# One unbroken TensorE visit per chunk for the recurrent part of a gated linear attention and gated MLP kernel

## Chip, cores and metric

One core of a Trainium2 chip. The metric is the device time of one launch in microseconds; the time shown for a kernel is the median of its runs.

## What is computed

Gated linear attention over 4 batches, 8 heads, 768 steps and head size 48, then a gated MLP with a convolution of three taps along the sequence ("MoE" in the code):

```
state = f[:, :, t, :, None] * state + einsum('bhd,bhe->bhde', k[:, :, t], v[:, :, t])   # f = sigmoid(f_logit)
y[:, :, t] = einsum('bhd,bhde->bhe', q[:, :, t], state)
...
h = maximum(x @ w_in, 0)                # x: y with the heads side by side, 384 wide; h: 1024 wide
conv_out = sum over k of conv_w[k] * hp[:, k:k+S, :]
out = (h * sigmoid(conv_out)) @ w_out
```

## The kernel before

The sequence is cut into 24 chunks of 128 steps, six to a batch. Chunk n goes through these steps; P is 128, NP the 4 pairs of heads, D the head size.

- `load_f`, `gate`, `load_kq`, `load_v` (lines 155 to 188): loads on SP's queue, and the logarithm of the gates on ScalarE (for later chunks three at a time, with a low part from GpSimd, line 175).
- `stage_a` (190): a matmul with a triangle sums the log gates (`pl`, 195), ScalarE takes both exponentials (199, 200), VectorE scales the keys (212), GpSimd the queries (213).
- `decay_out`, `decay_in` (216, 221): from chunk 5 on the last row of decays goes to DRAM and back, transposed, into `ft_all`.
- `stage_b` (229): four transposes each of keys and queries on TensorE (`ptk`, `ptq`, 235) and their copies out of PSUM into `kT` and `qT` (237): ScalarE, but for the keys of chunks 12 to 23 VectorE.
- `scores` (247): 8 matmuls of keys against queries, contraction 48, into `pa` (253); VectorE's masked copy into `am` (255).
- `state` (257): the rank update, 8 matmuls of keys against values into `pk` (266); VectorE adds the old state and multiplies with the decay (276, 277), which gives the state for chunk n+1. A batch's last chunk has none.
- `values` (279): the state part, 4 matmuls of state against queries (288; not at a batch's first chunk but the very first), and the score part, 8 matmuls of values against `am` (291), both summed in `py`. ScalarE and VectorE split the result in a high and a low part (299, 300) for the MLP.

Each matmul of plain fp32 is two instructions in the trace, so that a scores block is 16, a rank update 16, a state part 8, a score part 16, the transposes 4 and 4 (one instruction each).

The MLP works on half batches (three chunks). `mm1` (310): for each of 8 blocks of 128 hidden units a sum of 9 matmuls of 384 columns into `ph` (328), ScalarE's eviction (331), the convolution and the gate on both engines (333 to 343). `mm2` (345): for each 128 rows the high and low part of the gate's product (358, 359), a sum of 24 matmuls into `po` (365), eviction (368) and store (369). `ph` and `po` share two PSUM buffers; `pl`, `ptk`, `ptq` and `pk` share three; `pa` and `py` have one each.

The order of the work: every step is entered with a key by `plan` (383), mostly the chunk's number plus an offset of CFG, and is traced in the order of keys. The builder then goes through the traced program with its own model of times and gives each engine, whenever that is free, the instruction traced earliest among those whose inputs and buffers are ready in the model. The order on each engine is fixed by that when the kernel is built. A step that becomes ready can so come between two instructions of a step with a later key. On the chip each engine takes its instructions in this order and waits for semaphores.

The change touches `stage_b`, `scores`, `state`, `values` and the keys of lines 400 to 403. Before, these are:

```python
        plan(n - CFG["b"], lambda n=n: decay_out(n))          # b = 0.8
        plan(n - CFG["b"] + 0.4, lambda n=n: decay_in(n))
        plan(n, lambda n=n: scores(n))
        plan(n + CFG["s"], lambda n=n: state(n))              # s = 0.2
        plan(n + CFG["v"], lambda n=n: values(n))             # v = 0.5
```

The keys of `mm1` and `mm2` (lines 413 to 418) put the MLP of a half batch one to three half batches behind its attention; after the last chunk some MLP work remains alone.

Of the kernel before, what the change touches and what calls it, by code (L numbers as in the profile page):

```python
# [1 line left out]

# [7 lines left out]
F32 = mybir.dt.float32  # L10
# [7 lines left out]
P = 128  # L18
# [1 line left out]
F64_HI = float(np.uint32((1151 << 20) - 1).view(np.float32))  # L20

F_MIN = 2.0 ** -64
CFG = dict(groups=[3, 3, 3, 3, 3, 3, 3, 3], sg=3, f1=2.6, g1=2.6, gv=2, gl=5.2, g=3.9, l=3.2, a=1.8, b=0.8, s=0.2, v=0.5, wil=(-2.3, -1.1), wis=(-0.7, 0.9), cw=1.3, wol=(1.3, 1.0), wos=2.1, wo=0.35, m1=0.5, m1s=0.9, m2=1.5, m2s=1.2, ek=(12, 24), ec='d', er='p', tp=0, tf=2, nw=2, gd=0, q0=2, lf=3, kpool=2, eg='d', eq='p', es='d', em='d', ew='p', xb=3, nf=6, fe='a', kb=4, qb=3, vb=4, lv=2.2, cb=1, sb=3, fi=1)

@with_exitstack
def gla_moe_kernel(ctx, tc, q_in, k_in, v_in, f_in, w_in, conv_w, w_out, out):


    nc = tc.nc
    B, S, H, D = v_in.shape  # L30
    DM, DFF = w_in.shape
    q, k, v, f_logit = [t.rearrange("b s h d -> b h s d")[:, :, :, :D] for t in (q_in, k_in, v_in, f_in)]
    NC = S // P
    NP = H // 2
# [3 lines left out]
    CPH = NC // 2  # L38
    groups = CFG["groups"]
    GC = max(groups)  # L40
# [3 lines left out]
    HP = 64  # L44
# [7 lines left out]
    wk = fast.enter_context(tc.tile_pool(name="wk", bufs=2))  # L52
# [15 lines left out]
    mask = mask1.rearrange("p (j n t) -> p j n t", j=1, n=1).broadcast_to([P, 2, NP, P])  # L68

    def zeroed(shape, n, name, eng):  # L70
        ts = [wk.tile(shape, F32, name=f"{name}{i}", bufs=1) for i in range(n)]
        for t in ts:
            eng.memset(t, 0.0)
        return ts

    kp_b = [wk.tile([P, H, HP], F32, name=f"kp{i}", bufs=1) for i in range(CFG["kb"])]
    qp_b = [wk.tile([P, H, HP], F32, name=f"qp{i}", bufs=1) for i in range(CFG["qb"])]
    a_b = zeroed([P, 2, NP, P], 2, "am", nc.vector)
    s_b = zeroed([P, NP, HP + D], 2, "st", nc.vector)
# [6 lines left out]
    wo = const.tile([P, NF, 2, DM], F32R, name="wo")  # L86
    cw = const.tile([P, 3, NF], F32, name="cw")
# [30 lines left out]
    def raw_out(f):  # L118
        i = f // 4
        if ("o", i) not in raws:  # L120
            raws["o", i] = (wk.tile([P, 4, 2 * DM], I32, tag="g32", name=f"wos{i}") if i == 0 else
                            wk.tile([P, 4, 2 * DM], I32, tag="xT", name=f"wos{i}", bufs=CFG["xb"]))
        return raws["o", i][:, f % 4]
# [26 lines left out]

    last_exp = [None]
    group_of = [g for g, m in enumerate(groups) for _ in range(m)]
    ghl, gates, fbs, qkv, mid, tts, fts, ft_row = {}, {}, {}, {}, {}, {}, {}, {}

    def load_f(n):
        b, c = steps[n]
# [5 lines left out]
    def gate(g, i, m):  # L162

        if g >= CFG["lf"] and i == 0:
            ghl[g] = [wk.tile([P, GC, DM], F32R, tag=f"cg{x}", name=f"cg{x}{g}", bufs=CFG["cb"]) for x in "hl"]
        cs = slice(i * DM, (i + m) * DM)
# [49 lines left out]
    def decay_out(n):  # L216
        if n in fts:
            ft_row[n] = dr.tile([1, DM], F32, tag="ft", name=f"ft{n}", bufs=2)
            nc.sync.dma_start(ft_row[n], fts.pop(n)[P - 1:P].rearrange("o h d -> o (h d)"))

    def decay_in(n):

        if n in ft_row:
            b, c = steps[n]
            src = ft_row.pop(n).rearrange("o (p j d) -> j d (o p)", j=2, d=D)
            for j in range(2):
                nc.sync.dma_start(ft_all[HP * j:HP * j + D, b, c, :], src[j])

    def stage_b(n):
        qp, kp = mid.pop(n)  # L230
        tt = []
        for nm, src in (("k", kp), ("q", qp)):
            pt = ps.tile([P, NP, P], F32, tag="s", name=f"pt{nm}{n}", bufs=3)
            for p in range(NP):
                nc.tensor.transpose(pt[:, p, :], src[:, 2 * p:2 * p + 2, :].rearrange("p h d -> p (h d)"), ident)  # L235
            st = wk.tile([P, NP, P], F32, tag=f"{nm}T", name=f"{nm}T{n}")
            (nc.vector.tensor_copy if nm == "k" and CFG["ek"][0] <= n < CFG["ek"][1] else nc.scalar.copy)(st, pt)  # L237
            tt.append(st)
        tts[n] = (kp, tt[0], tt[1])

# [3 lines left out]
        nc.tensor.matmul(pw, zr[:, :P], zr, start=True, stop=True)  # L244
    xts = {}

    def scores(n):
        kp, kT, qT = tts[n]
        pa = ps.tile([P, 2, NP, P], F32, tag="A", name=f"pa{n}")
        for p in range(NP):  # L250
            for j in range(2):
                r = slice(HP * j, HP * j + D)
                nc.tensor.matmul(pa[:, j, p, :], kT[r, p, :], qT[r, p, :], start=True, stop=True)  # L253
        am = a_b[n % 2]
        nc.vector.copy_predicated(am, mask, pa)  # L255

    def state(n):
        b, c = steps[n]
        if c == NC - 1:
            return  # L260
        kp, kT, qT = tts[n]
        vt = qkv[n]
        pk = ps.tile([P, NP, D], F32, tag="s", name=f"pk{n}", bufs=3)
        for p in range(NP):
            for j in range(2):
                nc.tensor.matmul(pk[HP * j:HP * j + D, p, :], kp[:, 2 * p + j, :D], vt[:, 2 * p + j, :],  # L266
                                 start=True, stop=True)
        for j in range(2):
            r = slice(HP * j, HP * j + D)
            ft = ft_all[r, b, c, :].rearrange("p (n o) -> p n o", o=1).broadcast_to([D, NP, D])  # L270
            new = s_b[(n + 1) % 2][r, :, HP * j:HP * j + D]
            if c == 0:
                nc.vector.tensor_tensor(new, pk[r], ft, ALU.mult)
            else:
                tmp = wk.tile([P, NP, D], F32, tag="stmp", name=f"stmp{n}_{j}", bufs=1)
                nc.vector.tensor_tensor(tmp[r], pk[r], s_b[n % 2][r, :, HP * j:HP * j + D], ALU.add)
                (nc.vector if CFG["es"] == "d" else nc.gpsimd).tensor_tensor(new, tmp[r], ft, ALU.mult)

    def values(n):
        b, c = steps[n]  # L280
        kp, kT, qT = tts.pop(n)
        vt = qkv.pop(n)
        am = a_b[n % 2]
        py = ps.tile([P, NP, P], F32, tag="Y", name=f"py{n}")
        inter = c > 0 or n == 0
        if inter:
            for p in range(NP):
                nc.tensor.matmul(py[:HP + D, p, :], s_b[n % 2][:, p, :], qT[:, p, :], start=(p == 0), stop=False)  # L288
        for p in range(NP):
            for j in range(2):  # L290
                nc.tensor.matmul(py[HP * j:HP * j + D, p, :], vt[:, 2 * p + j, :], am[:, j, p, :],  # L291
                                 start=not inter and p == 0, stop=(p == NP - 1))
        hf = c // CPH
        if c % CPH == 0:
            xts[b, hf] = wk.tile([P, NP, 2, HS], F32R, tag="xT", name=f"xT{b}_{hf}", bufs=CFG["xb"])
        xT = xts[b, hf]
        ts = slice((c % CPH) * P, (c % CPH + 1) * P)
        for r in [slice(0, HP + D)] if c > 0 or n == 0 else [slice(0, D), slice(HP, HP + D)]:
            nc.scalar.copy(xT[r, :, 0, ts], py[r])  # L299
            nc.vector.tensor_tensor(xT[r, :, 1, ts], py[r], xT[r, :, 0, ts].bitcast(F32), ALU.subtract)  # L300
        if c % CPH == CPH - 1:
            for t in range(KT):
                for j in range(2):
                    s0, d0 = HP * j + GAP * t, HP * j + D
                    nc.sync.dma_start(xT[d0:d0 + GAP, t, :, :].bitcast(F32), xT[s0:s0 + GAP, KT, :, :].bitcast(F32))
# [77 lines left out]
    def plan(key, w):  # L383
        items.append((key, len(items), w))
# [10 lines left out]
    for n in range(N):  # L395
        plan(n - CFG["l"], lambda n=n: load_kq(n))
        plan(n - CFG["lv"], lambda n=n: load_v(n))
        plan(n - CFG["a"], lambda n=n: stage_a(n))
        plan(n - CFG["b"], lambda n=n: stage_b(n))
        plan(n - CFG["b"], lambda n=n: decay_out(n))  # L400
        plan(n - CFG["b"] + 0.4, lambda n=n: decay_in(n))
        plan(n, lambda n=n: scores(n))
        plan(n + CFG["s"], lambda n=n: state(n))
        plan(n + CFG["v"], lambda n=n: values(n))
    for i in range(DFF // WC):
        for kt in range(KT):
# [27 lines left out]
    with tc.If(n_ok < P * n_ft):  # L434
        with ExitStack() as slow:
            wk = slow.enter_context(tc.tile_pool(name="swk", bufs=2))
# [11 lines left out]
            st = wk.tile([P, DG, D], F32, name="sst", bufs=1)  # L448
            nc.gpsimd.memset(st, 0.0)
            for t0 in range(0, S, TB):  # L450
# [7 lines left out]
                fb, qb, kb = grouped(f_logit, "f"), grouped(q, "q"), grouped(k, "k")  # L458
                vb = wk.tile([P, TB, D], F32, tag="sv", name=f"sv{t0}")
# [22 lines left out]
                for t in range(0, TB, 8):  # L482
                    py = ps.tile([B * H, 8, D], F32, tag="sy", name=f"spy{t0}_{t}", bufs=2)
# [14 lines left out]
            for u in range(2 * B):  # L498
                b, hf = u // 2, u % 2
# [59 lines left out]
```

## Time and profile before

| what | us |
|---|---|
| median of 3 runs (lowest, highest) | 383.01 (381.41, 386.15) |
| the profiled execution, its own time | 384.77 |
| its span, first to last instruction | 383.1 |
| TensorE busy | 351.2 (92%) |
| TensorE loading weights | 313.2 (82%) |
| VectorE busy | 294.4 (77%) |
| ScalarE busy | 239.9 (63%) |
| GpSimd busy | 60.1 (16%) |

The profile is of one execution, and its rows below are from that. Busy matmul time is modelled from starts and sizes: a matmul that waits inside the array counts as busy. The time that a block costs is therefore read as the distance from its start to the start of the next block. PE is TensorE, PEld its weight loads, DVE VectorE, ACT ScalarE, POOL GpSimd, SP the engine that issues the transfers.

### The profile page before, as it was taken

The numbers are of one execution on the slowest core, as the hardware profiler recorded it, in microseconds if no ns is written. First come the engines' busy times: TensorE is split into PE (matmuls) and PEld (weight loads), VectorE is DVE, ScalarE is ACT, GpSimd is POOL, SyncE is SP. The second block draws the span as 40 slices with busy tenths as digits, with TensorE's granted clock in tenths as the row PEclk, the third lists the DMA queues.
The fourth block names the chain that finished last, engine by engine and source line by source line (L and its number), as shares of the span: only waits on it lengthen the run. The fifth ranks groups of instructions, "written<-read, shape, count | busy, mean of one in ns | idle before, by whom it ended". The sixth has DMA issues, their size and how long they took to land.

```text
span 383.1 us, 7239 instructions
## 1 busy us (share of the span) xinstructions
PE 351.2 (92%) x2735; PEld 313.2 (82%) x2735; DVE 294.4 (77%) x467; ACT 239.9 (63%) x426; POOL 60.1 (16%) x72
## 2 busy tenths in 40 slices
PE   5578799868989699999999999999999999999993
PEld 1557578746978599989989999999989899999993
DVE  3999999988989968667688896669869776575620
ACT  3687669993997376645875665547545555566530
POOL 1111134311103701104011121204101100000000
PEclk9989999996999989999999999999999999999998
DMA  7999253324334330132313332232201000201011
GB/s 224 347 366 362 83 164 105 89 59 104 105 76 108 75 114 21 50 90 87 113 56 99 75 81 83 69 87 74 66 22 34 21 2 21 54 21 43 21 44 49
DMA packets 28854, 36.04 MB, mean 94 GB/s; under 512 B 10847, under 2 KB 20106, under 8 KB 28810
## 3 DMA queue, kind: packets, MB, share of 16 engines
q1 hardware_dynamic: 28810, 35.49, 31.0%
q8 instruction: 24, 0.39, 0.4%
q14 instruction: 20, 0.16, 0.2%
HBM read 28.37 MB, written 4.75 MB: 86 GB/s over the span
## 4 chain that ended last, share of the span: by engine, by line
PE 60%; DVE 13%; ACT 9%; issue 5%; DMA 5%; POOL 3%; SPq 2%; ACTq 0%; POOLq 0%; DVEq 0%
PE po L365 23%; PE ph L328 21%; PE pa L253 4%; PE py L291 4%; DMA fb<-in_f_logit_dram 4%; PE py L288 3%; POOL cgl L175 3%; PE ptk L235 2%; PE ptq L235 1%; PE pl L195 1%; ACT fb L169 1%; DVE g L340 1%; PE pk L266 1%; ACT g L342 1%; DVE am L255 1%
## 5 line engine op out<-in xcount | busy, mean ns | idle before, releaser
L328 PE MATMUL ph<-xT,wi 128*128 128x384 f32 x576 | 116.4, 349 | 4.8 <-ACT hb L331 2.7
L328 PEld LDWEIGHTS ph<-xT,wi 128*128 128x128 f32 x576 | 100.0, 189 | 10.4 <-issue 3.9
L365 PE MATMUL po<-wo,gh 128*128 128x384 f32 x384 | 101.3, 345 | 0.0
L365 PEld LDWEIGHTS po<-wo,gh 128*128 128x128 f32 x384 | 69.9, 191 | 1.2 <-issue 0.7
L365 PE MATMUL po<-wo,gl 128*128 128x384 f32 x192 | 65.8, 343 | 1.3 <-DVE gl L359 1.3
L339 DVE SCALAR_TENSOR_TENSOR g<-hb,cw,g 128x384 f32<-128x384 f32 (+1 forms) x64 | 41.0, 640 | 15.5 <-ACT g L333 15.1
L359 DVE TENSOR_TENSOR gl<-g,gh 128x1024 fp32r<-128x1024 f32 (+4 forms) x34 | 31.4, 934 | 27.1 <-ACT gh L358 27.0
L331 ACT ACTIVATE hb<-ph 128x384 f32<-128x384 f32 x64 | 31.3, 489 | 31.3 <-PE ph L328 31.2
L213 POOL TENSOR_TENSOR qp<-qp,fd 128x384 f32<-128x384 f32 x22 | 31.5, 1430 | 99.4 <-ACT fd L200 95.0
L340 DVE SCALAR_TENSOR_TENSOR g<-hb,cw,g 128x384 f32<-128x384 f32 (+1 forms) x64 | 44.2, 690 | 1.9
L343 DVE SCALAR_TENSOR_TENSOR g<-g,hb 128x768 f32<-128x768 f32 (+1 forms) x32 | 31.4, 981 | 14.6 <-ACT g L342 14.3
L342 ACT ACTIVATE g<-g 128x768 f32<-128x768 f32 (+1 forms) x32 | 27.1, 848 | 24.3 <-DVE g L340 24.3
L358 ACT CAST gh<-g 128x1024 fp32r<-128x1024 f32 (+4 forms) x34 | 26.5, 800 | 23.7 <-PE po L365 20.6
L333 ACT ACTIVATE g<-hb,cw 128x384 f32<-128x384 f32 (+1 forms) x64 | 39.6, 618 | 2.0
L365 PEld LDWEIGHTS po<-wo,gl 128*128 128x128 f32 x192 | 36.6, 191 | 1.7 <-DVE gl L359 1.5
L253 PE MATMUL pa<-qT,kT 48*128 48x128 f32 x384 | 32.8, 298 | 1.2 <-ACT qT L237 1.1
L253 PEld LDWEIGHTS pa<-qT,kT 48*128 48x128 f32 x384 | 26.1, 195 | 9.5 <-issue 5.5
L255 DVE COPY_PREDICATED am<-mask,pa 128x1024 f32<-128x1024 uint8 x24 | 31.4, 1309 | 1.2 <-PE pa L253 1.1
L291 PE MATMUL py<-am,v 128*48 128x128 f32 x384 | 27.4, 284 | 1.1 <-DVE am L255 0.9
L288 PE MATMUL py<-qT,st 128*112 128x128 f32 x168 | 24.1, 283 | 2.6 <-DVE xT L300 1.6
L291 PEld LDWEIGHTS py<-am,v 128*48 128x48 f32 x384 | 20.6, 126 | 6.1 <-DVE am L255 2.0
L299 ACT CAST xT<-py 112x512 fp32r<-112x512 f32 (+1 forms) x27 | 15.8, 585 | 15.0 <-PE py L291 11.6
(92 smaller groups left out, 428.5 us busy)
## 6 DMA issues: line engine op xcount, KB each, us to landing
kp<-in_k_dram SPq DMA_DIRECT2D x24, 256.0 KB
qp<-in_q_dram SPq DMA_DIRECT2D x24, 256.0 KB
fb<-in_f_logit_dram SPq DMA_DIRECT2D x24, 192.0 KB
v<-in_v_dram SPq DMA_DIRECT2D x24, 192.0 KB
out_dram<-ob SPq DMA_DIRECT2D x24, 192.0 KB
wis<-in_moe_w_in_dram SPq DMA_DIRECT2D x6, 512.0 KB
wos<-in_moe_w_out_dram SPq DMA_DIRECT2D x8, 384.0 KB
xT<-xT SPq DMA_DIRECT2D x48, 48.0 KB
```

Of the source, the lines that this page charges most:

```text
L213: (nc.vector if CFG["eq"] == "d" or n < CFG["q0"] else nc.gpsimd).tensor_tensor(qp[:, :, :D], qp[:, :, :D], fd, ALU.mult)
L253: nc.tensor.matmul(pa[:, j, p, :], kT[r, p, :], qT[r, p, :], start=True, stop=True)
L255: nc.vector.copy_predicated(am, mask, pa)
L288: nc.tensor.matmul(py[:HP + D, p, :], s_b[n % 2][:, p, :], qT[:, p, :], start=(p == 0), stop=False)
L291: nc.tensor.matmul(py[HP * j:HP * j + D, p, :], vt[:, 2 * p + j, :], am[:, j, p, :], start=not inter and p == 0, stop=(p == NP - 1))
L328: nc.tensor.matmul(ph, wi[:, t, wl, f * P:(f + 1) * P], xts[b, hf][:, t, xl, :], start=(i == 0), stop=(i == 3 * KT - 1))
L333: nc.scalar.activation(cv, hb[:, 1:n + 1], AF.Copy, scale=cw[:, 1, f:f + 1])
L339: nc.vector.scalar_tensor_tensor(cv, hb[:, 2:n + 2], cw[:, 2, f:f + 1], cv, ALU.mult, ALU.add)
L340: nc.vector.scalar_tensor_tensor(cv, hb[:, 0:n], cw[:, 0, f:f + 1], cv, ALU.mult, ALU.add)
L343: nc.vector.scalar_tensor_tensor(cv, cv, 1.0, h_b[:, fp:fp + 2, 1:n + 1], ALU.add, ALU.mult)
L359: nc.vector.tensor_tensor(lo, g[:, f:f + k], hi.bitcast(F32), ALU.subtract)
L365: nc.tensor.matmul(po, g[:, f, :], wo[:, f, wl, :], start=(i == 0), stop=(i == 3 * NF - 1))
```

## The change

A visit of chunk n is made of the state part and score part of chunk n, the rank update of chunk n+1 and the scores of chunk n+1, in this order. From chunk 8 on (`ng`) the matmuls of each part are traced with a priority 4000 places ahead (`hp`). The first matmul of a visit gets a dependence on all copies into `kT` and `qT` of chunks n and n+1 and on the masked copy of chunk n; the first matmul of the rank update and of the scores gets an order edge, without a wait, behind the last matmul of the part before. `scores` and `state` of chunk n+1 get keys just behind `values` of chunk n. `decay_out` goes from 0.8 to 1.2 chunks ahead, `decay_in` from 0.4 to 0.7, for all chunks. The number of buffers of `kT` and `qT` becomes a setting (`tb`), at 2 as before.

```diff
-CFG = dict(groups=...
+CFG = dict(ng=8, hp=4000, tb=2, groups=...
...
-            st = wk.tile([P, NP, P], F32, tag=f"{nm}T", name=f"{nm}T{n}")
-            (nc.vector.tensor_copy if ... else nc.scalar.copy)(st, pt)
+            st = wk.tile([P, NP, P], F32, tag=f"{nm}T", name=f"{nm}T{n}", bufs=CFG["tb"])
+            i = (nc.vector.tensor_copy if ... else nc.scalar.copy)(st, pt)
+            ready.setdefault(n, []).append(i.ins)
...
+    NOSYNC = mybir.DependencyInfo(mybir.DependencyClass.NoSync, mybir.DependencyReason.DATA)
+    DATA = mybir.DependencyInfo(mybir.DependencyClass.Sync, mybir.DependencyReason.DATA)
+    last_pe = [None]
+
+    @contextmanager
+    def visit(n, part):
+        if n < CFG["ng"]:
+            yield
+            return
+        traced = nc.cur_bb.bb.instructions
+        start = len(traced)
+        with tc.high_priority(offset=CFG["hp"]):
+            yield
+        mine = traced[start:]
+        if part == 0:
+            for i in ready[n] + ready.get(n + 1, []):
+                tc.add_manual_dep(mine[0], i.name, DATA, reason="visit")
+        else:
+            tc.add_manual_dep(mine[0], last_pe[0].name, NOSYNC, reason="visit")
+        last_pe[0] = mine[-1]
...
     def scores(n):
-        for p in range(NP):
+        with visit(n - 1, 2):
+            for p in range(NP):
...
-        nc.vector.copy_predicated(am, mask, pa)
+        ready.setdefault(n, []).append(nc.vector.copy_predicated(am, mask, pa).ins)
...
     def state(n):
-        for p in range(NP):
+        with visit(n - 1, 1):
+            for p in range(NP):
...
     def values(n):
-        if inter:
+        with visit(n, 0):
+            if inter:
...
-        plan(n - CFG["b"], lambda n=n: decay_out(n))
-        plan(n - CFG["b"] + 0.4, lambda n=n: decay_in(n))
-        plan(n, lambda n=n: scores(n))
-        plan(n + CFG["s"], lambda n=n: state(n))
+        plan(n - 1.2, lambda n=n: decay_out(n))
+        plan(n - 0.7, lambda n=n: decay_in(n))
+        plan(n - 1 + CFG["v"] + 0.02 if n > CFG["ng"] else n, lambda n=n: scores(n))
+        plan(n - 1 + CFG["v"] + 0.01 if n > CFG["ng"] else n + CFG["s"], lambda n=n: state(n))
```

## Rows read from the trace of the kernel before

**Rows 1.** Two stretches: window, length, busy us of each engine, clock, DMA share, GB/s.
```profile
core 0: us, PE busy (x) PEld busy (x) DVE busy (x) ACT busy (x) POOL busy (x), PEclk, DMA share, GB/s
104.00:138.00 34.00, 29.34 (x232) 25.56 (x231) 31.76 (x48) 24.05 (x40) 11.05 (x8) 0.95 0.38 104
138.00:328.00 190.00, 189.81 (x1499) 174.66 (x1498) 145.39 (x207) 114.05 (x190) 27.31 (x34) 1.00 0.22 60
```

**Rows 2.** Waits of TensorE, 104 to 138 us: total us, times, longest us.
```profile
PE ptq L235 <- POOL qp L213: 1.7, 1, 1.7
PE po L365 <- DVE gl L359: 1.3, 1, 1.3
```

**Rows 3.** Waits of TensorE, 138 to 330 us, all of them.
```profile
PE ph L328 <- ACT ob L368: 0.2, 1, 0.2
```

**Rows 4.** Timeline of TensorE: start us, us, engine, line, what, count; whole blocks.
```profile
290.51 1.16 PE L253 MATMUL pa<-qT,kT 48*128 48x128 f32 x16
291.61 0.56 PE L266 MATMUL pk<-v,kp 128*48 128x48 f32 x16
292.10 0.66 PE L235 MATMUL ptk<-ident,kp 128*128 128x128 f32 x4
292.60 0.60 PE L235 MATMUL ptq<-ident,qp 128*128 128x128 f32 x4
```

**Rows 5.** Timeline of TensorE, a score part, then scores in two pieces.
```profile
245.63 1.08 PE L291 MATMUL py<-am,v 128*48 128x128 f32 x16
246.65 1.85 PE L328 MATMUL ph<-xT,wi 128*128 128x384 f32 x9
248.42 0.49 PE L253 MATMUL pa<-qT,kT 48*128 48x128 f32 x4
248.84 1.85 PE L328 MATMUL ph<-xT,wi 128*128 128x384 f32 x9
250.63 0.94 PE L253 MATMUL pa<-qT,kT 48*128 48x128 f32 x12
251.50 0.56 PE L266 MATMUL pk<-v,kp 128*48 128x48 f32 x16
```

**Rows 6.** Timeline of TensorE, a rank update in two pieces.
```profile
261.42 0.38 PE L266 MATMUL pk<-v,kp 128*48 128x48 f32 x8
261.73 3.44 PE L328 MATMUL ph<-xT,wi 128*128 128x384 f32 x18
265.11 0.39 PE L266 MATMUL pk<-v,kp 128*48 128x48 f32 x8
265.42 0.66 PE L235 MATMUL ptk<-ident,kp 128*128 128x128 f32 x4
```

**Rows 7.** Timeline of TensorE, 36 MoE matmuls and the next.
```profile
334.61 6.52 PE L328 MATMUL ph<-xT,wi 128*128 128x384 f32 x36
340.96 0.52 PE L365 MATMUL po<-wo,gh 128*128 128x384 f32 x2
```

**Rows 8.** Line 253, 138 to 328 us: count, ns min/median/max, first and last start.
```profile
L253 PE MATMUL pa<-qT,kT x208: 272/272/374, 146.1 to 318.7; 48*128 48x128 f32 x104
L253 PEldq EVENT_SEMAPHORE  x4: 51/51/51, 175.9 to 314.6; - x4
```

**Rows 9.** Timeline of TensorE, a score part with a rank update behind it.
```profile
101.75 1.08 PE L291 MATMUL py<-am,v 128*48 128x128 f32 x16
102.66 0.34 PE L266 MATMUL pk<-v,kp 128*48 128x48 f32 x6
```

**Rows 10.** Timelines of TensorE, ScalarE and VectorE: transposes of chunk 14, late copies.
```profile
183.93 0.60 PE L235 MATMUL ptq<-ident,qp 128*128 128x128 f32 x4
...
188.49 0.57 ACT L237 COPY qT<-ptq 128x512 f32<-128x512 f32 x1
...
294.33 0.67 DVE L237 COPY kT<-ptk 128x512 f32<-128x512 f32 x1
```

**Rows 11.** Timeline of ScalarE: the eviction that frees the buffer for 261.73.
```profile
259.88 0.48 ACT L368 COPY ob<-po 128x384 f32<-128x384 f32 x1
```

**Rows 12.** Waits of SP's queue, one line: total us, times, longest us.
```profile
SPq L227 <- DMA ft<-fd: 14.3, 15, 3.0
```

More of the change, by code (lines that the diff above doesn't have):

```diff
@@ L1 @@
-from contextlib import ExitStack
+from contextlib import ExitStack, contextmanager
 import numpy as np
@@ L22 @@
 F_MIN = 2.0 ** -64
-CFG = dict(groups=[3, 3, 3, 3, 3, 3, 3, 3], sg=3, f1=2.6, g1=2.6, gv=2, gl=5.2, g=3.9, l=3.2, a=1.8, b=0.8, s=0.2, v=0.5, wil=(-2.3, -1.1), wis=(-0.7, 0.9), cw=1.3, wol=(1.3, 1.0), wos=2.1, wo=0.35, m1=0.5, m1s=0.9, m2=1.5, m2s=1.2, ek=(12, 24), ec='d', er='p', tp=0, tf=2, nw=2, gd=0, q0=2, lf=3, kpool=2, eg='d', eq='p', es='d', em='d', ew='p', xb=3, nf=6, fe='a', kb=4, qb=3, vb=4, lv=2.2, cb=1, sb=3, fi=1)
+CFG = dict(ng=8, hp=4000, tb=2, groups=[3, 3, 3, 3, 3, 3, 3, 3], sg=3, f1=2.6, g1=2.6, gv=2, gl=5.2, g=3.9, l=3.2, a=1.8, b=0.8, s=0.2, v=0.5, wil=(-2.3, -1.1), wis=(-0.7, 0.9), cw=1.3, wol=(1.3, 1.0), wos=2.1, wo=0.35, m1=0.5, m1s=0.9, m2=1.5, m2s=1.2, ek=(12, 24), ec='d', er='p', tp=0, tf=2, nw=2, gd=0, q0=2, lf=3, kpool=2, eg='d', eq='p', es='d', em='d', ew='p', xb=3, nf=6, fe='a', kb=4, qb=3, vb=4, lv=2.2, cb=1, sb=3, fi=1)
 @with_exitstack
@@ L152, in gla_moe_kernel @@
     group_of = [g for g, m in enumerate(groups) for _ in range(m)]
-    ghl, gates, fbs, qkv, mid, tts, fts, ft_row = {}, {}, {}, {}, {}, {}, {}, {}
+    ghl, gates, fbs, qkv, mid, tts, fts, ft_row, ready = {}, {}, {}, {}, {}, {}, {}, {}, {}
     def load_f(n):
@@ L235, in stage_b @@
                 nc.tensor.transpose(pt[:, p, :], src[:, 2 * p:2 * p + 2, :].rearrange("p h d -> p (h d)"), ident)
-            st = wk.tile([P, NP, P], F32, tag=f"{nm}T", name=f"{nm}T{n}")
-            (nc.vector.tensor_copy if nm == "k" and CFG["ek"][0] <= n < CFG["ek"][1] else nc.scalar.copy)(st, pt)
+            st = wk.tile([P, NP, P], F32, tag=f"{nm}T", name=f"{nm}T{n}", bufs=CFG["tb"])
+            i = (nc.vector.tensor_copy if nm == "k" and CFG["ek"][0] <= n < CFG["ek"][1] else nc.scalar.copy)(st, pt)
+            ready.setdefault(n, []).append(i.ins)
             tt.append(st)
@@ L249, in scores @@
         pa = ps.tile([P, 2, NP, P], F32, tag="A", name=f"pa{n}")
-        for p in range(NP):
-            for j in range(2):
-                r = slice(HP * j, HP * j + D)
-                nc.tensor.matmul(pa[:, j, p, :], kT[r, p, :], qT[r, p, :], start=True, stop=True)
+        with visit(n - 1, 2):
+            for p in range(NP):
+                for j in range(2):
+                    r = slice(HP * j, HP * j + D)
+                    nc.tensor.matmul(pa[:, j, p, :], kT[r, p, :], qT[r, p, :], start=True, stop=True)
         am = a_b[n % 2]
-        nc.vector.copy_predicated(am, mask, pa)
+        ready.setdefault(n, []).append(nc.vector.copy_predicated(am, mask, pa).ins)
     def state(n):
@@ L263, in state @@
         pk = ps.tile([P, NP, D], F32, tag="s", name=f"pk{n}", bufs=3)
-        for p in range(NP):
-            for j in range(2):
-                nc.tensor.matmul(pk[HP * j:HP * j + D, p, :], kp[:, 2 * p + j, :D], vt[:, 2 * p + j, :],
-                                 start=True, stop=True)
+        with visit(n - 1, 1):
+            for p in range(NP):
+                for j in range(2):
+                    nc.tensor.matmul(pk[HP * j:HP * j + D, p, :], kp[:, 2 * p + j, :D], vt[:, 2 * p + j, :],
+                                     start=True, stop=True)
         for j in range(2):
@@ L285, in values @@
         inter = c > 0 or n == 0
-        if inter:
+        with visit(n, 0):
+            if inter:
+                for p in range(NP):
+                    nc.tensor.matmul(py[:HP + D, p, :], s_b[n % 2][:, p, :], qT[:, p, :], start=(p == 0), stop=False)
             for p in range(NP):
[L288 to L292, printed above, removed]
+                for j in range(2):
+                    nc.tensor.matmul(py[HP * j:HP * j + D, p, :], vt[:, 2 * p + j, :], am[:, j, p, :],
+                                     start=not inter and p == 0, stop=(p == NP - 1))
         hf = c // CPH
```

## Prediction

> **What bounds the kernel now.** I read the busy times by stretch first, then the waits of TensorE, then TensorE's timeline from 100 us to the end, then the timelines of ScalarE and VectorE where transposed keys are copied. In [rows 1] the reader is to see that TensorE is busy 189.81 of the 190 us from 138 to 328, at full clock, while VectorE has 145.39 us of work there: 44.6 us of room. From 104 to 138 TensorE does stand still (29.34 of 34 us, clock 0.95); the longest of those waits are in [rows 2]. After 138 one wait of 0.2 us is all that is left [rows 3]. After 328 only MoE matmuls follow, back to back [rows 7]. So the changed stretch (the first visit, chunk 8, stands near 105) is bound by the time TensorE needs for its own instructions, and an input that comes earlier gains nothing there. What can be gained is what the order of the instructions costs.
>
> That cost is read from starts, because the busy share counts a matmul that waits in the array as busy. A MoE group of 9 in a pure stretch takes (340.96 - 334.61) / 36 x 9 = 1.59 us [rows 7]. Between a score part and a scores block the same 9 take 248.42 - 246.65 = 1.77 us, and between two pieces of a scores block 250.63 - 248.84 = 1.79 us [rows 5]. Crossing from the attention forms to the MoE form and back costs 0.19 us.
>
> **The change, part by part.**
>
> *Cuts that go.* A scores block of 16 takes 291.61 - 290.51 = 1.10 us whole [rows 4]. Cut in 4 and 12 it takes 0.42 + 0.87 = 1.29 us, and the group put in between pays a crossing [rows 5]: 0.19 + 0.19 = 0.38 us for one cut. A rank update takes 0.49 us whole [rows 4], 0.31 + 0.31 cut in two [rows 6]: 0.13 + 0.19 = 0.32 us. From 138 to 328 the 208 matmuls of the scores [rows 8] are 13 blocks, and the timeline has them in 19 pieces; the 10 rank updates lie in 15 pieces, the 14 score parts in 16, the 12 state parts in 14. The diff ties a visit's parts with order edges and lifts them 4000 places, so MoE work cannot come between them. 6 x 0.38 + 5 x 0.32 = 3.9 us; the 2 score parts, priced like scores, 0.8; the state parts, whose form is the full array's, nothing. Sum 4.7 us.
>
> *Borders that go.* Before, score part and scores are two islands among MoE work; afterwards they are one, and of a crossing the half that enters the scores goes: 0.1 us. A score part followed by MoE takes 246.65 - 245.63 = 1.02 us [rows 5], one followed at once by a rank update 102.66 - 101.75 = 0.91 [rows 9]: another 0.1. The transposes keep their own way out. 13 x 0.2 = 2.6 us.
>
> *From 104 to 138* lie one cut of scores, two of rank updates and two chunks' borders: 0.38 + 2 x 0.32 + 0.4 = 1.4 us. The waits of [rows 2] come from GpSimd's scaled queries and from VectorE's low parts, which the diff does not touch: I leave them.
>
> [...]
>
> *The wait that is added.* A visit's first matmul waits for both copies of chunk n+1 as well as those of n and the masked scores. Its own cost: a further wait is a semaphore instruction of 51 ns on the weight queue [rows 8]; 16 x 0.05 = 0.8 us, taken in full; from below it is zero. If the copies are late, everything queued behind waits: all MoE matmuls, hence ScalarE's evictions and then VectorE. The copies of chunk 22 were done at 294.33 + 0.67 = 295.00, 1.8 us after its transposes (292.60 + 0.60) [rows 4, 10]; those of chunk 14 at 189.06, 4.5 us after theirs at 183.93 + 0.60 = 184.53 [rows 10]. Today several groups of other work stand between the copies and the scores. With the lift, the builder puts a visit where its own model has the copies done, so the slack comes down to the difference of model and chip. Bounds per visit: 0, and 4.5 us. The nearest evidence is the places where the builder cut a block because a MoE group had just become ready: such a start is as tight as a visit's will be. At 261.73 the group cuts a rank update [rows 6]; its buffer was free at 259.88 + 0.48 = 260.36 [rows 11], so the chip had 1.37 us in hand. I take 0 us.
>
> *Moved with it.* Scores and rank update, which in [rows 5] begin 2.8 and 5.9 us after the score part, now follow it at once. Their VectorE work (mask, two additions, two products) is unchanged in amount and has the 44.6 us of room; were that gone, its queue would hold the gate chain and then MoE's second product. The decay row's two transfers are planned 0.4 and 0.3 chunk earlier; on SP the loads and stores behind them wait for the first to land, 14.3 us over 15 waits, 3.0 at most [rows 12]. Loads are planned over two chunks ahead, which covers this: 0, at worst one 3.0 us wait. The product with the decay now comes as soon as a score part (0.91 us) and a rank update (0.49 us) after the copies; a late landing would hold VectorE, again inside its room. The transposed tiles keep two buffers each, so nothing is lost or won there.
>
> *Sum.* 4.7 + 2.6 + 1.4 - 0.8 = 7.9 us. The profiled execution took 384.77 us for a span of 383.1, and would take 376.9; it stands 1.8 us above the median of the three runs, 383.01, to which the forecast is tied: 375.1 us.
>
> **The rivals.**
>
> *Smaller gain.* Only the borders are saved: what a piece itself loses comes back, because a visit's first matmul, held by its wait, starts as exposed as a cut piece does. 16 x 0.19 = 3.0 us back, 378.1 us. For it: a piece of scores loses just that [rows 5]. Against it: the parts behind the first run on without a gap [rows 9].
>
> *Slower.* The visits wait for late copies. The place is the first matmul of each visit; the price is the wait times 16; it decides from 7.9 / 16 = 0.49 us, above which the kernel is slower than before. With 1.0 us each, 8.1 us over: 391.1 us. For it: copies 1.8 and 4.5 us behind the transposes, in queues that also hold the gates, and the lost cover. Against it: the 1.37 us above, and a single 0.2 us wait in 190 us. [...]
>
> *It does not do what it says.* Only the first matmul of a visit carries the list of inputs; if a later part lacks a buffer or an input (the rank update takes one of three buffers shared with the transposes), MoE work comes between after all, or the cuts move to the transposes. Then 383.0 us.
>
> *Larger gain.* The new order also avoids the two waits of 1.7 and 1.3 us [rows 2] and the low clock that follows (0.05 of 34 us, 1.7 us [rows 1]): 375.1 - 4.7 = 370.4 us. Nothing in the diff aims at it.
>
> **How the numbers follow.** Forecast 0.45, smaller gain 0.20, larger 0.12, no effect 0.10, slower 0.13. The time is 375.1. The range reaches from 369, a little below the larger gain, to 387, half way into the slower case; about 0.15 lies outside. The bounds of faster and slower by 2%, about what a measurement of this kernel can tell from no change, are 375.35 and 390.7. The first lies in the middle of the likeliest case, which I give 371 to 379: half of its 0.45 and nearly all of the larger gain are faster, 0.34; of the slower case all but a little is slower by over 2%, 0.11; the rest is 0.55.
>
> **What would show it.** Right: state part, score part, rank update and scores in one unbroken row from chunk 8 on, scores never in pieces; a score part before a rank update near 0.91 us; fewer than 0.19 us a MoE group lost; the pure MoE tail unchanged in length but starting some 8 us sooner; TensorE's waits after 105 about as few as now. Wrong: waits of TensorE on the copies of keys or queries at the score or state part, above 0.5 us each; clock below 1.00 between 138 and 320; VectorE waiting for the decay row; blocks still in pieces.

## The result, and the profile after

The changed kernel took 381.36 us (median of 13 runs, 377.5 to 383.7), the kernel before beside it 384.38 (13 runs, 381.41 to 386.83). The ratio is 0.9896 with an interval of 0.9866 to 0.9926, all of it below 1. The gain is 1.0%, some 4 us by the ratio and 3.0 between the medians, where 2.06% (7.9 us) was forecast. The profiled execution took 381.93 us for a span of 380.1.

The windows view, same stretches as [rows 1]:

```profile
core 0: us, PE busy (x) PEld busy (x) DVE busy (x) ACT busy (x) POOL busy (x), PEclk, DMA share, GB/s
104.00:138.00 34.00, 27.74 (x251) 25.97 (x252) 32.33 (x50) 22.33 (x39) 6.16 (x7) 1.00 0.34 89
138.00:328.00 190.00, 185.72 (x1509) 178.28 (x1508) 147.81 (x209) 116.03 (x196) 26.06 (x35) 0.99 0.24 65
```

From 138 on more matmuls fit into the same 190 us (1509 against 1499), and TensorE still stands for 4.3 us of it where it stood for 0.2: it has waits there that it did not have before. From 104 to 138 it is busy for 27.74 us, 1.6 less than in [rows 1]. The waits of TensorE, first 104 to 150 us, then 150 to the end:

```profile
PE ph L354 <- ACT hb L357: 6.2, 2, 3.6
PE po L391 <- DVE gl L385: 2.7, 1, 2.7
...
PE ph L354 <- ACT ob L394: 1.0, 3, 0.4
PE ph L354 <- ACT hb L357: 0.7, 1, 0.7
```

Together 10.6 us; the kernel before has 4.8 from chunk 8 on, [rows 2 and 3] and three waits of 1.2, 0.3 and 0.2. None of the new ones stands at a visit. All stand at MLP work. The timeline of TensorE shows why for the first, the 3.60 us ahead of 112.39 ("the hole" below), and a visit behind it:

```profile
107.76 0.60 PE L235 MATMUL ptk<-ident,kp 128*128 128x128 f32 x4
108.20 0.60 PE L235 MATMUL ptq<-ident,qp 128*128 128x128 f32 x4
112.39 1.85 PE L354 MATMUL ph<-xT,wi 128*128 128x384 f32 x9 [3.60 <-ACT hb L357]
114.08 0.34 PE L195 MATMUL pl<-cgh,tri 128*128 128x384 f32 x1
114.26 0.34 PE L195 MATMUL pl<-cgl,tri 128*128 128x384 f32 x1
114.43 1.04 PE L314 MATMUL py<-qT,st 128*112 128x128 f32 x8
115.40 1.08 PE L317 MATMUL py<-am,v 128*48 128x128 f32 x16
116.31 0.53 PE L291 MATMUL pk<-v,kp 128*48 128x48 f32 x16
116.77 1.16 PE L277 MATMUL pa<-qT,kT 48*128 48x128 f32 x16
117.86 1.86 PE L354 MATMUL ph<-xT,wi 128*128 128x384 f32 x9
...
143.95 2.61 PE L354 MATMUL ph<-xT,wi 128*128 128x384 f32 x9 [2.58 <-ACT hb L357]
```

The four parts stand in one row, as every visit does from here on: score part 0.91 us (116.31 - 115.40), rank update 0.46, scores 1.09. That is the forecast picture. But the state and score part of chunk 8, 1.9 us, come behind the hole. Before, the same two blocks stood inside it, at 108.13, and left two waits of 0.30 and 1.19 us. The timeline of TensorE in the kernel before:

```profile
108.13 1.10 PE L288 MATMUL py<-qT,st 128*112 128x128 f32 x8 [0.30 <-DVE xT L300]
109.16 1.08 PE L291 MATMUL py<-am,v 128*48 128x128 f32 x16
111.43 1.85 PE L328 MATMUL ph<-xT,wi 128*128 128x384 f32 x9 [1.19 <-ACT hb L331]
```

In the changed kernel, the timeline of ScalarE over the same time, and over the wait at 143.95:

```profile
109.41 1.28 ACT L368 ACT_TABLE_LOAD   x1
110.71 0.84 ACT L368 ACTIVATE g<-g 128x770 f32<-128x770 f32 x1
111.46 0.49 ACT L107 CAST wo<-mswo 128x384 fp32r<-128x384 f32 x1
111.86 0.48 ACT L357 ACTIVATE hb<-ph 128x384 f32<-128x384 f32 x1
112.24 0.58 ACT L237 COPY kT<-ptk 128x512 f32<-128x512 f32 x1
112.71 0.60 ACT L237 COPY qT<-ptq 128x512 f32<-128x512 f32 x1
...
141.06 1.28 ACT L170 ACT_TABLE_LOAD   x1
142.35 1.16 ACT L170 ACTIVATE fb<-fb 128x1152 f32<-128x1152 f32 x1
143.42 0.47 ACT L357 ACTIVATE hb<-ph 128x384 f32<-128x384 f32 x1
```

From 104.99 to 113.19 ScalarE has the same order as in the kernel before from 104.03 to 112.22, and works without a gap (busy share 7.94 of 8 us from 104 to 112). The eviction that frees the MLP's buffer comes behind a table load, a gate and a split (111.86), and the copies that the visit now waits for (chunk 9's) come behind that eviction, done at 113.31. So the added wait was paid (the run "first half free" below shows how much of the hole it made), but not where the prediction looked for it: nothing waits at the visit's first matmul, since the builder, which knows of the wait, put MLP work in front; that work then waits with nothing left to fill the time. The transposes were done by 108.80 (108.20 + 0.60), and their copies, at 112.24 and 112.71, still came behind the table load, the gate, the split and the eviction.

**An account of the 273.89 us.** Executions reach chunk 8 up to 4 us apart though the code to there is the same, so lengths are taken between matched places, up to which two kernels have issued the same matmuls of every kind: from the start of chunk 8's scores (102.93 before, 103.89 after) to the start of TensorE's last MLP matmul (376.82, 374.25). "Idle" is TensorE's waiting in between; "slow" is one minus the granted clock, summed over windows of 1 us; "own" is the rest. Each row is one execution. The decay keys alone (below), with no visits either, have 0.6 us less of their own than the kernel before, so that differences of that size are not read.

| kernel | length | idle | slow | own | own against without visits |
|---|---|---|---|---|---|
| before | 273.89 | 4.84 | 1.7 | 267.3 | |
| decay keys alone, no visits | 274.98 | 4.79 | 3.4 | 266.8 | -0.6 |
| after, visits from 8 | 270.35 | 10.55 | 1.7 | 258.1 | -9.2, 0.58 a visit |
| from 9 | 270.71 | 8.57 | 3.4 | 258.7 | -8.6, 0.57 |
| from 11 | 269.11 | 6.27 | 1.7 | 261.1 | -6.2, 0.48 |
| from 15 | 270.19 | 5.04 | 1.7 | 263.4 | -3.9, 0.43 |
| first half free | 269.19 | 5.58 | 3.4 | 260.2 | -7.1, 0.45 |
| first half free, 8 to 10 only | 268.19 | 6.85 | 3.4 | 257.9 | -9.4, 0.59 |
| first half free, from 11 | 274.36 | 7.98 | 3.4 | 263.0 | -4.4, 0.34 |
| light, no visits | 261.89 | 1.23 | 0 | 260.7 | |
| light, from 8 | 261.94 | 5.91 | 1.7 | 254.3 | -6.3, 0.40 |
| light, from 11 | 259.03 | 3.07 | 0 | 256.0 | -4.7, 0.36 |

(The light kernels, below, are matched from an MLP matmul at 103.59 us of the one without visits.) After against before: own -9.2, idle +5.7, together -3.5. The saving is there in full, 1.3 us more than the 7.9 of the forecast, and more than half of it came back as waiting.

### The profile page after: what moved, and what is told of

Read it like the earlier page. It is cut to its first block, busy times and chain, and to the rows that moved or that the text cites. A ratio compares the mean times of both kernels' runs of the same rounds, so it can differ in the third digit from the quotient of the medians.

```text
span 380.1 us, 7247 instructions
## 1 busy us (share of the span) xinstructions
PE 345.7 (91%) x2735; PEld 317.8 (84%) x2735; DVE 296.3 (78%) x467; ACT 238.2 (63%) x426; POOL 53.1 (14%) x72
## 4 chain that ended last, share of the span: by engine, by line
PE 60%; ACT 13%; DVE 7%; DMA 7%; issue 7%; SPq 3%; POOL 2%; ACTq 0%; POOLq 0%; DVEq 0%
PE po L391 22%; PE ph L354 19%; PE py L317 4%; PE pa L277 4%; DMA fb<-in_f_logit_dram 4%; PE py L314 3%; DMA wis<-in_moe_w_in_dram 2%; PE ptq L235 2%; PE ptk L235 2%; DVE g L366 1%; PE pk L291 1%; PE pl L195 1%; DVE g L365 1%; ACT fb L170 1%; ACT fb L169 1%
## 5 line engine op out<-in xcount | busy, mean ns | idle before, releaser
L354 PE MATMUL ph<-xT,wi 128*128 128x384 f32 x576 | 115.1, 348 | 11.6 <-ACT hb L357 8.6
L354 PEld LDWEIGHTS ph<-xT,wi 128*128 128x128 f32 x576 | 101.4, 190 | 16.5 <-ACT hb L357 10.2
L391 PE MATMUL po<-wo,gh 128*128 128x384 f32 x384 | 99.4, 340 | 0.0
L365 DVE SCALAR_TENSOR_TENSOR g<-hb,cw,g 128x384 f32<-128x384 f32 (+1 forms) x64 | 42.7, 669 | 10.6 <-ACT g L359 10.0
L385 DVE TENSOR_TENSOR gl<-g,gh 128x1024 fp32r<-128x1024 f32 (+4 forms) x34 | 32.9, 978 | 16.6 <-ACT gh L384 16.4
L369 DVE SCALAR_TENSOR_TENSOR g<-g,hb 128x768 f32<-128x768 f32 (+1 forms) x32 | 30.6, 957 | 15.4 <-ACT g L368 15.4
L213 POOL TENSOR_TENSOR qp<-qp,fd 128x384 f32<-128x384 f32 x22 | 29.6, 1345 | 89.6 <-ACT fd L200 84.2
L277 PE MATMUL pa<-qT,kT 48*128 48x128 f32 x384 | 30.7, 299 | 0.9 <-ACT qT L237 0.8
L212 DVE TENSOR_TENSOR kp<-kp,fi 128x384 f32<-128x384 f32 x22 | 19.7, 895 | 9.6 <-ACT fi L199 9.6
L314 PE MATMUL py<-qT,st 128*112 128x128 f32 x168 | 25.4, 296 | 0.0
## 6 DMA issues: line engine op xcount, KB each, us to landing
kp<-in_k_dram SPq DMA_DIRECT2D x24, 256.0 KB
qp<-in_q_dram SPq DMA_DIRECT2D x24, 256.0 KB
```

The lines of the kernel that those rows point to most:

```text
L354: nc.tensor.matmul(ph, wi[:, t, wl, f * P:(f + 1) * P], xts[b, hf][:, t, xl, :], start=(i == 0), stop=(i == 3 * KT - 1))
L365: nc.vector.scalar_tensor_tensor(cv, hb[:, 2:n + 2], cw[:, 2, f:f + 1], cv, ALU.mult, ALU.add)
L369: nc.vector.scalar_tensor_tensor(cv, cv, 1.0, h_b[:, fp:fp + 2, 1:n + 1], ALU.add, ALU.mult)
L385: nc.vector.tensor_tensor(lo, g[:, f:f + k], hi.bitcast(F32), ALU.subtract)
L391: nc.tensor.matmul(po, g[:, f, :], wo[:, f, wl, :], start=(i == 0), stop=(i == 3 * NF - 1))
```

## Experiments

Two theories stood at first. A: between 104 and 150 us VectorE and ScalarE set the pace, attention pieces filled TensorE's waits there, and visits take these fillers away. B: the loss belongs to the first visit, or to its late eviction, wherever that is.

**Visits from chunk 11 on.**

```diff
-ng=8
+ng=11
```

> Visits begin at chunk 11 in place of 8. Theory A: between 104 and 150 us VectorE and ScalarE set the pace (the weight split, the gates, the activation tables), pieces of attention work fill TensorE's waits there, and visits 8 to 10 take these fillers away, so that what the order saves is given back. Then this kernel keeps the stretch up to 150 as in the kernel before (TensorE's waits from 104 to 150 about 4.7 us, not 8.9) and keeps the saving after 150: 5 to 6 us under the kernel before, ratio 0.984 to 0.987, some 2 us under the changed kernel. Theory B: the loss belongs to the first visits wherever they begin (attention run ahead leaves nothing to fill with behind it): waits of 4 us and more appear behind chunk 11, ratio 0.990 or above.

Measured: 379.69 us, ratio 0.9866 (0.9832 to 0.9900), in A's range. The longest waits of TensorE, 104 to 150 us:

```profile
PE ptq L235 <- POOL qp L213: 1.6, 1, 1.6
PE po L391 <- DVE gl L385: 1.3, 1, 1.3
PE ph L354 <- ACT hb L357: 1.2, 1, 1.2
```

These are the waits of the kernel before, and no hole stands ahead of the first visits, so a loss at the first visit wherever it begins falls. There are three visits fewer, and the length is 1.2 us shorter. (The interval of the time overlaps with the changed kernel's, so that the time alone does not show the difference.)

**First half free.** State and score part wait for chunk n's inputs only; rank update and scores for chunk n+1's; the order edges stay.

```diff
-        if part == 0:
-            for i in ready[n] + ready.get(n + 1, []):
-                tc.add_manual_dep(mine[0], i.name, DATA, ...)
-        else:
+        for i in ready[n] if part == 0 else ready[n + 1]:
+            tc.add_manual_dep(mine[0], i.name, DATA, ...)
+        if part:
```

> The state and score part of chunk n wait for chunk n's inputs alone; the copies of chunk n+1 are waited for at the rank update, or at the scores where there is none. Theory A: the wait of 3.6 us before the MoE group at 112 us in the changed kernel is there because chunk 8's state and score part, 2 us of work that the kernel before did in that hole, were held for the copies of chunk 9; freed, they go back into it, the hole shrinks to about 1.2 us, and 1.5 to 2 us are won over the changed kernel: ratio 0.984 to 0.986. After 150 us the visits may come apart in two, which costs at most 0.2 us each. Theory B: the hole comes from the late eviction alone and the order does not matter: the hole stays, ratio 0.988 to 0.992.

Measured: 379.57 us, ratio 0.986 (0.9818 to 0.9901): A's figure, but the interval reaches into B's. The trace decides. The timeline of TensorE at the hole, and at a later wait:

```profile
108.61 1.10 PE L313 MATMUL py<-qT,st 128*112 128x128 f32 x8 [0.30 <-DVE xT L325]
109.63 1.08 PE L316 MATMUL py<-am,v 128*48 128x128 f32 x16
111.90 1.86 PE L353 MATMUL ph<-xT,wi 128*128 128x384 f32 x9 [1.19 <-ACT hb L356]
...
131.17 0.69 PE L390 MATMUL po<-wo,gh 128*128 128x384 f32 x1 [1.57 <-DVE wo L109]
```

With the wait for chunk 9 taken from the first half, both blocks are back in the hole and 3.60 us shrink to 0.30 + 1.19. This shows that the added wait made the rest of it, 2.1 us.

**The keys of the decay row alone.** `ng=99`: no visits, the decays still planned earlier.

> No visits at all; only the earlier keys of the decay row's two transfers remain of the change. All theories: nothing, ratio 0.997 to 1.003. If it is 0.994 or below, part of the measured gain belongs to the decay keys and not to the visits.

Measured: 384.4 us, ratio 0.9979 (0.9954 to 1.0004). That part of the change does nothing that can be measured.

**Waits without the lift.** `hp=0`: the dependences and order edges stay, the priority goes.

> Visits with their waits and order edges, but without the lift of 4000 places. Theory A (the lift keeps MoE work out, the edges only fix the order among the parts): the blocks are in pieces again, more than in the kernel before since a whole visit can be interrupted anywhere; each piece costs 0.3 to 0.4 us as read from the kernel before; ratio 1.00 or above. Theory B (edges and waits are enough): blocks whole, ratio 0.988 to 0.992.

Measured: 419.76 us, ratio 1.0863 (1.0799 to 1.0926). The timeline of TensorE inside a score part:

```profile
201.08 0.42 PE L317 MATMUL py<-am,v 128*48 128x128 f32 x2
201.43 0.45 PE L391 MATMUL po<-wo,gh 128*128 128x384 f32 x1
201.81 0.42 PE L317 MATMUL py<-am,v 128*48 128x128 f32 x2
202.15 0.44 PE L391 MATMUL po<-wo,gl 128*128 128x384 f32 x1
```

The order edges bind only the first matmul of a part; the lift keeps it whole. Without it blocks fall into pairs with one MLP matmul between. A round takes 201.81 - 201.08 = 0.73 us; the same three instructions in whole blocks take 2 x 0.91 / 16 + 6.35 / 36 = 0.29 [rows 7]. So each such cut costs 0.44 us, a little above the 0.32 to 0.38 that the prediction puts on a cut. By the measure of the table the length is 35.1 us more than before: 27.5 of TensorE's own, 6.8 of slow clock, 0.8 of waiting. Without the lift the rest of the change makes the kernel slower; only with it are blocks whole.

**Lighter VectorE, without and with visits.** The low halves of w_out are left out (zeros, not worked out) in the kernel before and in the changed one; the matmuls with them still run.

```diff
+    nc.gpsimd.memset(wo[:, :, 1, :].bitcast(F32), 0.0)
...
+        if hi_only:
+            nc.scalar.copy(hi, mf)
+            return
```

> The kernel before, with one part of the computation left out: the low halves of w_out are zero (a GpSimd fill) and are not worked out, which takes some 8 x 2.4 = 19 us of work from VectorE, most of it between 60 and 135 us. Theory A (what the change lost between 104 and 150 us it lost because VectorE and ScalarE set the pace there): VectorE is no longer full in that stretch, and this kernel is the base for the next run; by itself it is 3 to 8 us faster than before (ratio 0.98 to 0.99), since TensorE's waits of 4.6 us there mostly go. Theory B (the loss belongs to the first visit and to its late eviction alone, whatever VectorE has to do): the same for this kernel; only the difference to the next run tells them apart.

> The changed kernel with the same part left out as in the run beside it (low halves of w_out zero and not worked out). Theory A: with VectorE's 19 us gone from the stretch the visits cost no waits there, and the full gain of the visits shows: 5 to 8 us less than the run beside it (ratio to before about 0.015 to 0.02 lower than that run's). Theory B: the gain over the run beside it stays at about 3 us (0.008 lower), with the hole ahead of the second visit still there.

Measured: 374.74 us, ratio 0.9751 (0.9708 to 0.9794), and 374.83 us, 0.9736 (0.9703 to 0.9769). Of the visits' gain nothing is left that can be measured. Both theories missed: A wanted it wider, B unchanged. The light kernel without visits was also faster than its expectation (0.98 to 0.99). The waits of TensorE, 104 to 150 us, first without visits:

```profile
PE ph L332 <- ACT ob L372: 1.2, 1, 1.2
```

then with them:

```profile
PE ph L358 <- ACT ob L398: 2.2, 1, 2.2
PE py L318 <- ACT qT L241: 1.1, 1, 1.1
PE pl L199 <- DVE stmp L305: 0.6, 1, 0.6
PE po L395 <- ACT hb L361: 0.4, 1, 0.4
```

The edit freed the kernel before from its waits, so that all 4.7 us of added idle, and 1.7 of slow clock behind it, are the visits' doing. It is a weaker test than meant: VectorE's work fell by 11.7 us in all (294.4 to 282.7) where 19 were expected, and in 104 to 150 VectorE fell only from 40.1 to 37.9 us of 46, and ScalarE did not fall at all (34.5 and 34.9). The second row is a visit that does wait for a late copy, the event of the slower rival.

From this came theory C: the visits of chunks 8 to 10 lose it, whatever VectorE has to do, since their order leaves the chains through ScalarE and VectorE uncovered.

**Light, visits from chunk 11 on.** The light edit with `ng=11`.

> Visits from chunk 11 on (ng = 11), with the low halves of w_out zero and not worked out, as in the two light kernels (0.9751 without visits, 0.9736 with visits from chunk 8). In that pair VectorE had room and the visits still lost their whole gain: of the positions that both reach, the one with visits was 3.3 us further behind between 106 and 152 us and won 3.3 us afterwards. Theory C (the three visits of chunks 8 to 10 lose it, whatever VectorE has to do, because their order leaves the chains of ScalarE and VectorE uncovered): without them no wait over 1.5 us between 104 and 150, some 13 x 0.48 - 1.7 = 4.5 us less than without visits, ratio 0.961 to 0.966. Theory D (with a light VectorE there is little to save by visits at any place): 0.971 to 0.976.

Measured: 371.98 us, ratio 0.9652 (0.9622 to 0.9683), in C's range and clear of D's. The waits of TensorE, 104 to 150 us:

```profile
PE ph L358 <- ACT ob L398: 1.0, 1, 1.0
```

Leaving out three visits gains what sixteen did not: against the light kernel with visits from 8 some 0.9%, with the intervals apart.

**Visits from chunk 9 on.** `ng=9`.

> Visits from the tenth chunk on (ng = 9), the full computation. The hole of 3.6 us ahead of the second visit should shrink to the 1.2 us of the kernel before, as the score part of chunk 8 can fill it again. Theory C (each of the visits of chunks 8 to 10 takes a filler away): the waits of 2.7 and 2.6 us between 129 and 147 stay, ratio 0.986 to 0.989. Theory E (only the first visit's wait for the copies of chunk 9 costs): waits between 104 and 150 fall to about 5 us, ratio 0.983 to 0.986, as good as from chunk 11 or better.

Measured: 381.3 us, ratio 0.9902 (0.9873 to 0.9932); E falls, and C's range is just missed on the slow side. The waits of TensorE, 104 to 150 us, the three longest:

```profile
PE po L391 <- DVE wo L109: 2.0, 1, 2.0
PE pl L195 <- ACT kT L237: 1.5, 1, 1.5
PE ph L354 <- ACT hb L357: 1.2, 1, 1.2
```

The hole is down to 1.2 us as foretold, but other waits have come between 128 and 134 us, of other sizes and releasers than the expectation named, and a longer stretch of slow clock behind them (3.4 us lost in place of 1.7).

**Visits from chunk 15 on.** `ng=15`.

> Visits from the sixteenth chunk on (ng = 15), nine instead of sixteen, all of them in the stretch where TensorE is the bound. If each visit there is worth the 0.48 us that the run from chunk 11 showed (6.2 us of own time over 13 visits), 9 x 0.48 = 4.3 us, less 0.4 us of waits: ratio 0.989 to 0.991. The waits of 1.3 us on ScalarE's evictions between 175 and 205 should be gone, if visits bring them; if they stay, they are not of the visits' making.

Measured: 381.37 us, ratio 0.9898 (0.9863 to 0.9933). Nine visits give what sixteen gave. After 150 us the waits view of TensorE has one row left:

```profile
PE ph L354 <- ACT ob L394: 0.4, 1, 0.4
```

so the three waits of the changed kernel between 180 and 205 us were of the visits' making too.

**Visits from the first chunk on.** `ng=0`.

> Visits from the first chunk on (ng = 0) instead of the ninth. Before 104 us TensorE is busy for about half of the stretch and waits for loads and for both elementwise engines. Theory A (a visit pays only where TensorE sets the pace, and takes fillers away elsewhere): the whole order saves little or nothing more ahead of chunk 8, and more waits stand between 50 and 150 us; ratio 0.990 to 1.01. Theory B (only one first visit pays): the hole moves to the first chunks, where TensorE waits anyway, so nothing is lost at 105 to 112 and the ratio is 0.983 to 0.987.

Measured: 382.4 us, ratio 0.9918 (0.9885 to 0.995), in A's range. (In the kernel before TensorE was busy for 82.92 of the first 104 us, well over the half of the expectation.) TensorE reaches the matched place of 104.96 us at 112.26, later than any other run did, and is 8.5 us quicker from there: what visits cost ahead of chunk 8 takes back most of what they give (part of the late arrival can be the spread of 4 us between executions).

**First half free for chunks 8 to 10, whole waits from 11 on.**

```diff
+        wait = ready[n] + (ready.get(n + 1, []) if n >= 11 else [])
+        for i in wait if part == 0 else ready[n + 1] if n < 11 else []:
```

> Visits from the ninth chunk on, but the first visits (chunks 8 to 10) wait for their own chunk's inputs only, the parts of the next chunk for theirs; from chunk 11 on the visit waits for all. It puts together the two edits that each gave 0.986. Theory A: the loss between 104 and 150 us shrinks as with the free first half, and after 150 us the blocks lie whole as in the changed kernel: 0.980 to 0.986, at least as fast as either. Theory B (one mend takes back all that there is to take back at the first visit): 0.986, no better than either alone.

Measured: 380.5 us, ratio 0.9887 (0.9846 to 0.9929). The time is neither theory's figure and decides nothing. The trace says more. TensorE's own time is that of the changed kernel (257.9 and 258.1 us), and its waiting is 6.85 us in place of 10.55. The waits of TensorE, 104 to 150 us, the three longest of 4.9 us in all, where the changed kernel has 8.9:

```profile
PE po L391 <- DVE wo L109: 1.6, 1, 1.6
PE ptk L235 <- DVE kp L212: 1.3, 2, 0.8
PE ph L354 <- ACT hb L357: 1.2, 1, 1.2
```

So in this execution 3.7 of the 5.7 us of added waiting are gone with the visits kept and only the wait for the next chunk's copies moved, in three visits. Slow clock took 1.7 us of that back. By this trace the loss that theory C puts on the order of the visits of chunks 8 to 10 is for the larger part that of the added wait in them.

**First half free, from chunk 11 on.** `ng=11` and the diff of "first half free".

> Both edits that each gave 0.986 to 0.987: visits from chunk 11 on, and their first half (state part, score part) waits only for its own chunk's inputs, the second half for the next chunk's. Theory C (what is lost after 150 us, 1.3 to 1.7 us of waits, comes from TensorE's visits being unbroken, and is smaller when the halves may stand apart, but a visit in two halves has one more border): waits after 150 us fall to 0.7 us or less, and the time is that of from chunk 11, less at most 1 us: 0.983 to 0.987. If the free first half is what matters for the whole, 0.980 to 0.983; if the halves that stand apart cost a border each (13 x 0.1 to 0.2 us), 0.988 to 0.990.

Measured: 384.53 us, ratio 1.0008 (0.9975 to 1.0041): the whole gain gone, outside all three expectations. The waits of TensorE after 150 us:

```profile
PE po L390 <- ACT hb L356: 1.8, 1, 1.8
PE py L313 <- DVE am L278: 1.6, 2, 1.0
```

and the windows view behind the first of them, with a granted clock of 0.57:

```profile
191.00:195.00 4.00, 3.39 (x11) 3.39 (x12) 3.72 (x7) 2.17 (x5) 0.10 (x1) 0.57 0.00 0
```

By the table, against "from 11": 1.8 us more of its own (a second border for each of 13 visits, 0.14 each), 1.7 of waiting, 1.7 of slow clock. As I read it, visits in halves issue the scores later, and the first half then waits for the masked copy (second row above); no run tests that. Two mends that help alone do not add up.

## Why the prediction was wrong

The direction and the work saved were right; the gain came to two fifths to a half of the forecast's. Point by point:

- *Cuts that go* and *borders that go*: right. From 138 to 328 every block of the changed kernel is whole: scores in 13 pieces (19 before), rank updates in 10 (15), score parts in 14 (16), state parts in 12 (14). From a matched place at 155.36 us (157.63 after) to one at 328.59 (326.00) the kernel gains 4.86 us with 1.51 more idle, 6.4 us of its own. The steps give 4.7 + 2.6 less 13 semaphores of 0.05, 6.65, for the somewhat longer stretch from 138. The price of nothing for the cuts of the state parts rests on their form in the prediction, which no run shows to be the reason; the price itself agrees with the trace of the kernel before, where the state part begun at 267.94 takes 268.51 - 267.94 = 0.57 and 273.43 - 273.12 = 0.31 us in its two pieces, 0.88 in all, a whole one 285.78 - 284.81 = 0.97, and the two MLP matmuls behind the first piece 268.94 - 268.51 = 0.43, 0.08 more than two of [rows 7]. Ahead of it the own saving was 2.9 us, where *from 104 to 138* had 1.4; why it is more is not shown. The marks named for "right" are all there but two: the tail starts 2.6 us sooner (338.39 against 340.96 in [rows 7]) and not some 8, and waits after 105 are not as few as before.
- *What bounds the kernel now* is the step that failed, in the sentence "So the changed stretch (the first visit, chunk 8, stands near 105) is bound by the time TensorE needs for its own instructions, and an input that comes earlier gains nothing there", with "I leave them" on the waits of [rows 2]. [Rows 1] stood beside it: 29.34 busy of 34 us, VectorE 31.76. In that stretch the order of TensorE decides how much of the chains through ScalarE and VectorE is covered, and the change rewrites the order. Idle went from 4.84 to 10.55 us, a loss for which the sum has nothing: 9.2 saved less 5.7 of waiting is the 3.5 us by which the length fell. Of the 5.7, 4.2 lie ahead of the matched place at 155.36. The runs show where: visits only from 11 on keep the old waits there, visits of chunks 8 to 10 bring the new ones, with the full and with the light work.
- *The wait that is added*: "I take 0 us" holds at the visit (no visit of the changed kernel waits) and fails as a price. In the first hole it cost 2.1 us, shown by the free first half; moved in the visits of chunks 8 to 10 alone, it takes 3.7 of the 5.7 us away. So this price of 0 is the term that failed, together with the bound. I asked whether the copies would be late for the visit, not what else TensorE would have to do until then.
- *Slower*: its mechanism, late copies, acted in the first hole (2.1 us, through the work in front of the visit) and, in the light kernel, at a visit itself (1.1 us), but not at each of sixteen.
- *Larger gain* went the other way: instead of avoiding the two waits of [rows 2] the order made longer ones. The slow clock that follows moved from 134 to 144 us and cost the same 1.7 us.
- *Smaller gain* gives 378.1, nearer to the median, but by a mechanism that did not act: the pieces' loss did not come back.

What stays open: why each single wait of 104 to 150 falls where it does. The builder orders everything anew with every edit, so that waits move between edits (chunk 9 and the free first half show it). That a third buffer for the MLP's sums would cover them was not tried. Visits from 11 on (0.9866) and the free first half from 8 on (0.986) have the best ratios of the full kernels; their intervals overlap with the changed kernel's, so that either is only likely to be better. With the light work, "from 11" beats "from 8" clearly.

## What to carry to other kernels

Ask of each stretch by itself whether the engine you reorder is its bound; here a busy share of 86% with an elementwise engine at 93% said no. There a block that is ready fills a wait, and holding it back for an unbroken visit loses the filler: without the visits of chunks 8 to 10 the length was 1.2 us shorter in the full kernel and 2.9 in the light one. A wait added to a block can be paid by what the builder puts in front of it (here 2.1 of the 3.60 us ahead of 112.39): look for its price at the neighbours, not at the block. Where the engine is the bound, count blocks kept whole: here 0.34 to 0.59 us a visit.

## What was not expected of the hardware

TensorE's granted clock, around some of its waits, was 0.50 for a while. Of the changed kernel, behind the wait of 2.58 us that ended at 143.95:

```profile
145.00:148.00 3.00, 3.00 (x13) 2.92 (x12) 1.09 (x2) 2.99 (x7) 1.01 (x1) 0.50 0.00 1
```

Each such stretch took 1.7 us, or twice that, as the column "slow" has it. It did not follow every wait (none behind the 3.60 us at 112.39; one behind 1.77 us in the last experiment), so I can price it only after the fact.
